# Attention and two expert layers in one kernel: four chunks ahead instead of two, and gathers in another order

## The chip, the cores and the metric

One core of a Trainium2 chip runs the whole kernel in one launch. The metric is the device time of one execution in microseconds (us), as the median of several. The engines are named as in the profile: PE is TensorE (matrix products; PEld is its loading of weights), DVE is VectorE, ACT is ScalarE, POOL is GpSimd, and SP is the engine whose queue issues the plain transfers.

## The reference

Three parts follow one another; each takes the result of the one ahead.

```python
# 1 sliding-window attention: 4 batches, 8 heads, 576 positions, head 64, window 64
scores = np.where(mask, scale * (q @ k.T), -1e9)     # mask: 0 <= i - j < 64
x = softmax(scores) @ v                              # -> x, 2304 tokens x 512
# 2 "moe": one dense layer
h = x @ w_in                                         # 512 -> 2048
x = (h - np.tanh(h)) @ w_out                         # 2048 -> 512
# 3 "moe2": eight experts, each token goes to one
logits = xn @ en.T / tau                             # normalised rows, 8 experts
e, gate = argmax(logits), softmax(logits)[argmax]
out = gate * (np.maximum(x @ w1[e], 0) @ w2[e])      # 512 -> 1024 -> 512
```

w_in and w_out come as 64-bit floating-point words, so a block of them takes twice the bytes and has to be decoded on the chip.

## The kernel before

Products are made of 32-bit numbers that are split into a high and a low part: one product of the reference becomes three on TensorE (`mm3`: high by high, high by low, low by high; lines 596 to 598). The splitting is work of its own: a copy to the high part (L222, on ScalarE or VectorE) and a subtraction for the low part (L572 for x, L393 and L862 for weights, L662 for the hidden layer).

The 2304 tokens lie in nine chunks of 256 (`CT`). Attention (`t_attn`) runs in units of half a chunk, n = 0 to 17; its result is x transposed. For the chunks in `direct` it goes straight into a buffer of pool "x" on the chip (two such buffers); for every other visit of a chunk it is spilled to `xTd` in DRAM (L552) and later loaded again (`t_xload`, L581) into one of four staging buffers "st", and split.

The dense layer has 16 blocks of 128 hidden units (`KF`). A *slot* is one chunk by one block: 12 products of 128x256 (`mm1`: x by w_in) and 6 of 128x512 (`mm2`: hidden layer by w_out). `t_moe1` takes two blocks, a *pair*, at once: `mm1`, then a chain of five ScalarE and five VectorE operations (VectorE's are L635, L644, L648, L652 and last the low part L662), then `mm2`. The weights of a block stay in one of 16 "w" slots until all chunks that use it have passed; loading and decoding a block (`t_decode`: loads L345 and L350, five VectorE operations L364, L367, L373, L378, L393 on each half) goes on during the first stage, and so does attention. Since the weights of the early stage are not there at once, the list `order` visits the first four chunks in pieces, (chunk, first block, last block), and puts away partial sums between: `t_sum` loads the sum so far (L687), adds (L694), and stores it (L699) to `part`. Chunks 4 to 8 then go through all 16 blocks. After its last block a chunk is routed (`t_route`, L700 to L844): it writes its rows to `x2d` and, for each token, its place in the list of its expert, `lst`.

The experts follow in an order that the chip works out. For each there is a first block of 256 tokens ("v" buffers) and an overflow block ("g" buffers): `t_list` loads the list of tokens (L1177 for the overflow part, L1179 for the first), `t_gather` gathers their rows on GpSimd (L908, two gathers of 128 rows a block), `t_xin` and `t_xin1` transpose them on TensorE (L931, L1030) and split them, `t_p1` and `t_ffn` do the products, `t_out` scatters (L1017). The overflow block stands in a branch on the token count. The counts are read into registers by eight `values_load` (L1280), one for each expert, on all engines.

No loop of the program sets the order: `Sched` takes all tasks with their engine, cost and due time (`prio`) and simulates them while the program is built; what its clock says is ready goes out, earliest due time first. It writes one list of instructions for each engine. Its costs for transfers (`SAME[DMA]`, `MOVED`) and the slot times `TC` and `TM` set what it believes, and so the order.

Of the kernel before, what the change touches and what calls it, by code (L numbers as in the profile page):

```python
# [40 lines left out]
class Sched:  # L41
# [3 lines left out]
    SAME = {PE: 0.0, ACT: 0.14, DVE: 0.13, POOL: 0.15, DMA: 0.91}  # L45
    OTHER, MOVED = 0.21, 0.91
# [51 lines left out]
    def run(self):  # L98
# [11 lines left out]
        while ready or ending:  # L110
            for i, (prio, n, alts, deps, bufs, allocs, lat, _) in enumerate(ready):
# [18 lines left out]
                if e == DMA:  # L130
                    issue = self.ISSUE_HALF if dur == HALF else self.ISSUE
                    self.free[e] = self.now + issue
                    end = self.moved = max(self.moved, self.now + issue + 0.65) + dur
# [28 lines left out]
def attn_moe_moe2(ctx, tc, q, k, v, w_in, w_out, emb, tau, w1, w2, out):  # L162

    nc = tc.nc
# [234 lines left out]

    def t_attn(n, pr, direct, spill):  # L400

# [136 lines left out]
        if direct:  # L538
            if p == 0:
                xT[c] = Buf("x")  # L540
# [17 lines left out]
    def t_split(x, part, src, key, d0, d1, pr, psum):  # L558
# [3 lines left out]
        def hi():  # L562
            return x.t[:, 0, d0:d1, :].rearrange("p a b -> p (a b)")

        def lo():
            return x.t[:, 1, d0:d1, :].rearrange("p a b -> p (a b)")
# [33 lines left out]
    def t_moe1(c, f, acc, first, last, pr):  # L600
# [4 lines left out]
        def mm1(i):  # L605
            w = wt[f + i]
            for d in range(KD):
# [3 lines left out]
                    hp.t[:, i * CT:(i + 1) * CT], w.t[:, s], w.t[:, s2], x.t[:, 0, d, :], x.t[:, 1, d, :],  # L611
# [612 lines left out]
    T0, TC, TM = 8, 4.5, 3.3  # L1224
# [6 lines left out]
    order = [(0, 0, 4), (1, 0, 4), (1, 4, 8), (0, 4, 8), (2, 0, 8), (3, 0, 8), (3, 8, 12), (2, 8, 12)]  # L1231
    order += [(2, 12, KF), (3, 12, KF), (0, 8, KF), (1, 8, KF)]
    order += [(c, 0, KF) for c in range(4, NC)]
    direct = (0, 1)
    AHEAD = 25
    start, due, load, held, s_ = {}, {}, [], [], 0
    for c, f0, f1 in order:
        load.append(c not in held and not (c in direct and f0 == 0))
        held = [x for x in held if x != c][-1:] + [c]
# [4 lines left out]
    t_weights(lambda f, o: due[f] - 6.0 + 3.0 * o)  # L1244
    for n in range(NC * NU):
        c = n // NU
        t_attn(
            n, min(TA * n, slot_t(start[c, 0]) - AHEAD + 5.0 * (n % NU)) if c else 1.0 * n, c in direct,
            any(l and x[0] == c for l, x in zip(load, order)),
        )  # L1250
    for (c, f0, f1), l in zip(order, load):
        if l:
            t_xload(c, slot_t(start[c, f0]) - 15.0)
# [5 lines left out]
        x2 = t_sum(c, acc, f0 > 0, f1 == KF, f1 - 5, end - 12.0 if c + 1 < NC else 0.0)  # L1259
# [12 lines left out]
    t_list(0, 1, fin - 50)  # L1272
    t_list(1, 0, fin - 49)
    t_counts(fin)
    blk_o = t_gather(lb[:, 0, 1], ("lb", 0, 1), "g", fin)
    blk_n = t_gather(lb[:, 1, 0], ("lb", 1, 0), "v", fin)
# [163 lines left out]
```

## Time and profile before

| | |
|---|---|
| median of 3 runs | 871.47 us (869.81 to 877.52) |
| the profiled execution | 870.94 us, its span 869.2 us |
| mean granted clock of TensorE | 0.97 of full speed |
| PE, PEld busy | 789.5 us (91%), 685.9 us (79%) |
| DVE, ACT busy | 592.5 us (68%), 502.3 us (58%) |
| POOL busy | 94.1 us (11%) |
| instructions | 15603 |
| moved | 107.2 MB, 123 GB/s |

An engine's busy time is the time in which the profiler saw at least one of its instructions at work. TensorE's products overlap, so the next one starts well ahead of the end that is shown. Where a row of the timeline has a bracket, the engine was idle for that long ahead of it, and the name behind the arrow is what ended the wait. In the view by stretches the columns are: the stretch, its length, busy time and number of instructions (x) of PE, PEld, DVE, ACT and POOL, the granted clock of TensorE as a share of full speed, the busy share of the DMA engines, and GB/s. About the first 330 us hold attention and the decoding of weights beside the dense layer, up to about 560 the dense layer is alone, and from then on the experts run.

### The profile page before, as it was taken

To read this page: it belongs to the slowest core of one execution; us is meant where nothing else is said; L and a number is where in the kernel's file an instruction comes from. 1 tells how busy PE (TensorE), PEld (TensorE's weight loads), DVE (VectorE), ACT (ScalarE), POOL (GpSimd) and SP (SyncE) were. 2 spreads that over 40 slices of the span, in tenths; PEclk is the share of its full clock that TensorE was granted. 3 is DMA by queue.
4 is the path that set the end of the run, shared out by engine and by line. 5 is a ranking of instruction groups with operands and counts; after the bars stand their busy time and mean duration, and the time that the engine had idled before them with its cause. 6 is when DMAs were issued, how large, how long until landed. Compare 5 with 4: busy or idle time off the path is not lost. (4 is left out here: it accounts for less than half of the span.)

```text
span 869.2 us, 15603 instructions
## 1 busy us (share of the span) xinstructions
PE 789.5 (91%) x5703; PEld 685.9 (79%) x5703; DVE 592.5 (68%) x1459; ACT 502.3 (58%) x1165; POOL 94.1 (11%) x116
## 2 busy tenths in 40 slices
PE   4687889999998999999999998895989999997995
PEld 3576678887987889899898987675879788886884
DVE  6998999999986796767667677951276377253721
ACT  6998798788955775656555556821244344242421
POOL 2000000000020110010101001022022123121210
PEclk9988899999999999999999999996999999998999
DMA  8964765447425310100100006615066266235411
GB/s 267 300 198 129 260 219 174 145 133 259 136 63 113 111 60 15 50 1 5 44 2 26 1 25 216 179 45 168 13 227 209 100 221 226 93 92 175 157 38 39
DMA packets 66284, 107.20 MB, mean 123 GB/s; under 512 B 8452, under 2 KB 44292, under 8 KB 66192
## 3 DMA queue, kind: packets, MB, share of 16 engines
q1 hardware_dynamic: 61296, 92.88, 33.1%
q0 software_dynamic: 4896, 13.13, 5.0%
q8 instruction: 53, 0.87, 0.5%
q14 instruction: 39, 0.32, 0.1%
HBM read 87.47 MB, written 19.56 MB: 123 GB/s over the span
## 5 line engine op out<-in xcount | busy, mean ns | idle before, releaser
L596 PE MATMUL h<-x,w 128*128 128x256 f32 x776 | 224.6, 289 | 10.0 <-DVE g L648 7.7
L598 PE MATMUL h<-x,w 128*128 128x256 f32 x776 | 221.4, 285 | 1.5 <-DVE w L393 1.5
L597 PE MATMUL h<-x,w 128*128 128x256 f32 x776 | 221.2, 285 | 1.2 <-DVE x L572 1.2
L596 PE MATMUL o<-w,gh 128*128 128x512 f32 x464 | 188.2, 406 | 11.2 <-ACT gh L658 10.2
L598 PE MATMUL o<-w,gh 128*128 128x512 f32 x464 | 184.5, 398 | 5.6 <-DVE gh L662 3.1
L597 PE MATMUL o<-w,gh 128*128 128x512 f32 x464 | 183.1, 395 | 0.0
L596 PEld LDWEIGHTS h<-x,w 128*128 128x128 f32 x776 | 149.9, 193 | 18.3 <-issue 9.8
L597 PEld LDWEIGHTS h<-x,w 128*128 128x128 f32 x776 | 150.0, 193 | 5.0 <-DVE x L572 1.4
L598 PEld LDWEIGHTS h<-x,w 128*128 128x128 f32 x776 | 150.0, 193 | 2.2 <-DVE w L393 2.1
L598 PEld LDWEIGHTS o<-w,gh 128*128 128x128 f32 x464 | 87.9, 189 | 33.5 <-DVE gh L662 7.6
L596 PEld LDWEIGHTS o<-w,gh 128*128 128x128 f32 x464 | 88.3, 190 | 29.5 <-ACT gh L658 11.2
L222 ACT CAST w<-st 128x512 fp32r<-128x512 f32 x140 | 83.0, 628 | 32.0 <-DMA st<-in_moe_w_dram 28.8
L597 PEld LDWEIGHTS o<-w,gh 128*128 128x128 f32 x464 | 88.4, 191 | 13.9
L862 DVE TENSOR_TENSOR w<-st,w 128x512 fp32r<-128x512 f32 x128 | 82.0, 686 | 6.0 <-ACT w L222 5.7
L658 ACT CAST gh<-g 128x512 fp32r<-128x512 f32 x72 | 44.3, 621 | 51.5 <-DVE g L652 46.6
L640 ACT ACTIVATE g<-h 128x512 f32<-128x512 f32 x72 | 43.1, 599 | 47.0 <-DVE g L644 42.0
L648 DVE TENSOR_TENSOR g<-h,g 128x512 f32<-128x512 f32 x72 | 49.6, 688 | 27.7 <-ACT g L640 26.9
L635 DVE SCALAR_TENSOR_TENSOR g<-g 128x512 f32<-128x512 f32 x72 | 49.9, 693 | 20.8 <-ACT g L627 20.4
L662 DVE TENSOR_TENSOR gh<-g,gh 128x512 fp32r<-128x512 f32 x72 | 49.3, 690 | 16.2 <-ACT gh L658 16.2
L644 DVE TENSOR_TENSOR g<-h,g 128x512 f32<-128x512 f32 x72 | 49.8, 691 | 9.9 <-ACT g L640 5.6
L482 ACT ACTIVATE pr<-pr,mx 128x128 f32<-128x128 f32 x144 | 56.2, 398 | 0.0
L652 DVE COPY_PREDICATED g<-big,g 128x512 f32<-128x512 uint16 x72 | 53.8, 748 | 1.0
(171 smaller groups left out, 1156.2 us busy)
## 6 DMA issues: line engine op xcount, KB each, us to landing
st<-in_moe_w_dram SPq DMA_DIRECT2D x64, 512.0 KB, 5.2
st<-in_moe_w_in_dram SPq DMA_DIRECT2D x16, 512.0 KB, 4.8
st<-in_moe_w_out_dram SPq DMA_DIRECT2D x16, 512.0 KB, 3.6
v<-in_v_dram SPq DMA_DIRECT2D x16, 512.0 KB, 5.1
k<-in_k_dram SPq DMA_DIRECT2D x16, 320.0 KB, 5.2
q<-in_q_dram SPq DMA_DIRECT2D x18, 256.0 KB, 4.0
xTd<-tmp SPq DMA_DIRECT2D x18, 256.0 KB, 4.2
st<-xTd SPq DMA_DIRECT2D x9, 512.0 KB, 4.4
```

The source lines that it names most:

```text
L222: return {ACT: (act, lambda: nc.scalar.copy(out=o(), in_=i())), DVE: (dve, lambda: nc.vector.tensor_copy(out=o(), in_=i()))}
L482: nc.scalar.activation(out=pr_.t[:, i, :], in_=pr_.t[:, i, :], func=AF.Exp, bias=st["m"][:, i:i + 1], scale=-1.0, accum_out=st["den"][:, i ...
L596: nc.tensor.matmul(out=ps, lhsT=ah, rhs=bh, start=start, stop=False)
L597: nc.tensor.matmul(out=ps, lhsT=ah, rhs=bl, start=False, stop=False)
L598: nc.tensor.matmul(out=ps, lhsT=al, rhs=bh, start=False, stop=stop)
L635: {DVE: (0.6, lambda: nc.vector.scalar_tensor_tensor(out=sq(), in0=sq(), scalar=SQ_B, in1=u(), op0=ALU.add, op1=ALU.mult))},
L644: {DVE: (0.6, lambda: nc.vector.tensor_tensor(out=sq(), in0=hp.t, in1=sq(), op=ALU.mult))},
L648: {DVE: (0.6, lambda: nc.vector.tensor_tensor(out=u(), in0=hp.t, in1=u(), op=ALU.subtract))},
L652: {DVE: (0.6, lambda: nc.vector.copy_predicated(out=sq(), mask=big.t.bitcast(DT.uint16), data=u()))},
L658: {ACT: (0.52, lambda: nc.scalar.copy(out=gh(), in_=sq()))}, reads=[(g, 1), (acc[0], "-"), (acc[1], "-")],
L662: {DVE: (0.6, lambda: nc.vector.tensor_tensor(out=gl(), in0=sq(), in1=gh().bitcast(F32), op=ALU.subtract))},
L862: return lambda: eng.tensor_tensor(out=w.t[:, b], in0=raw.t[:, a], in1=w.t[:, a].bitcast(F32), op=ALU.subtract)
```

## The change

Four chunks instead of two are worked on over the first four weight blocks with their x still on the chip. Chunks 0 and 1 have the two "x" buffers, chunks 2 and 3 take two of the 16 "w" slots for it, which `xv` views in the shape of x. After those four blocks the x of chunks 2 and 3 goes on to the second four, then 1 and 0; the third and fourth four blocks are visited in an order in which two chunks reload their x from `xTd` each time. The sums of the four chunks are put away more often: 12 stores and 12 loads of partial sums, where there were 8 of each. x is loaded nine times and spilled 18 times in both programs.

In the planner a transfer takes 1.2 times its duration and lands 1.5 after instead of 0.91; the slot times `TC` and `TM` are shorter, attention is due 10 ahead of its slot instead of 25, and x is loaded 12 ahead instead of 15. The gathers of expert 0 and 1 are asked for in another order: list and rows of expert 1's first block ("v") ahead of expert 0's overflow ("g"). One `values_load_multi_w_load_instructions` of all eight counts, planned as a task, stands where eight `values_load` followed the first part of the program.

```diff
-    SAME = {PE: 0.0, ACT: 0.14, DVE: 0.13, POOL: 0.15, DMA: 0.91}
-    OTHER, MOVED = 0.21, 0.91
+    SAME = {PE: 0.0, ACT: 0.14, DVE: 0.13, POOL: 0.15, DMA: 1.5}
+    OTHER, MOVED = 0.21, 1.5
...
-                    end = self.moved = max(self.moved, self.now + issue + 0.65) + dur
+                    end = self.moved = max(self.moved, self.now + issue + 0.65) + 1.2 * dur
...
+    def xv(x):
+        return x.t.rearrange("p (h k t) -> p h k t", h=2, k=KD) if x.pool == "w" else x.t
...
-                xT[c] = Buf("x")
+                xT[c] = Buf(direct)
...
-                    hp.t[:, i * CT:(i + 1) * CT], w.t[:, s], w.t[:, s2], x.t[:, 0, d, :], x.t[:, 1, d, :],
+                    hp.t[:, i * CT:(i + 1) * CT], w.t[:, s], w.t[:, s2], xv(x)[:, 0, d, :], xv(x)[:, 1, d, :],
...
-    T0, TC, TM = 8, 4.5, 3.3
+    T0, TC, TM = 8, 3.7, 2.9
...
-    order = [(0, 0, 4), (1, 0, 4), (1, 4, 8), (0, 4, 8), (2, 0, 8), (3, 0, 8), (3, 8, 12), (2, 8, 12)]
-    order += [(2, 12, KF), (3, 12, KF), (0, 8, KF), (1, 8, KF)]
-    order += [(c, 0, KF) for c in range(4, NC)]
-    direct = (0, 1)
-    AHEAD = 25
-    start, due, load, held, s_ = {}, {}, [], [], 0
-    for c, f0, f1 in order:
-        load.append(c not in held and not (c in direct and f0 == 0))
-        held = [x for x in held if x != c][-1:] + [c]
+    order = [(0, 0, 4, "x"), (1, 0, 4, "x"), (2, 0, 4, "w"), (3, 0, 4, "w"), (3, 4, 8, ""), (2, 4, 8, "")]
+    order += [(1, 4, 8, ""), (0, 4, 8, ""), (0, 8, 12, ""), (1, 8, 12, ""), (3, 8, 12, "load"), (2, 8, 12, "load")]
+    order += [(2, 12, KF, ""), (3, 12, KF, ""), (1, 12, KF, "load"), (0, 12, KF, "load")]
+    order += [(c, 0, KF, "load") for c in range(4, NC)]
+    AHEAD, LEAD, WLEAD = 10, 12.0, 6.0
+    start, due, s_ = {}, {}, 0
+    for c, f0, f1, how in order:
...
+        first = [x[3] for x in order if x[0] == c]
         t_attn(
             n, min(TA * n, slot_t(start[c, 0]) - AHEAD + 5.0 * (n % NU)) if c else 1.0 * n,
...
+            first[0] if first[0] != "load" else None, "load" in first,
         )
...
-            t_xload(c, slot_t(start[c, f0]) - 15.0)
+        if how == "load":
+            t_xload(c, slot_t(start[c, f0]) - LEAD)
...
-        x2 = t_sum(c, acc, f0 > 0, f1 == KF, f1 - 5, end - 12.0 if c + 1 < NC else 0.0)
+        x2 = t_sum(c, acc, f0 > 0, f1 == KF, f1 - 5 if f1 - 5 > f0 else f0, end - 12.0 if c + 1 < NC else 0.0)
...
-    t_list(0, 1, fin - 50)
-    t_list(1, 0, fin - 49)
+    t_list(1, 0, fin - 50)
+    t_list(0, 1, fin - 49)
     t_counts(fin)
-    blk_o = t_gather(lb[:, 0, 1], ("lb", 0, 1), "g", fin)
     blk_n = t_gather(lb[:, 1, 0], ("lb", 1, 0), "v", fin)
+    blk_o = t_gather(lb[:, 0, 1], ("lb", 0, 1), "g", fin + 2.0)
+    vals = []
+    SC.add(
+        {DVE: (0.3, lambda: vals.extend(
+            nc.values_load_multi_w_load_instructions(cnti[0:1, 0:E], min_val=0, max_val=NT)[1]))},
+        reads=[("cnt", 0), ("ids", blk_o[0][0])], prio=fin + 30.0,
+    )
...
-    vals = [nc.values_load(cnti[0:1, e:e + 1], min_val=0, max_val=NT) for e in range(E)]
```

In the changed program the lines of the kernel's body stand four to eight further down (L662 is L666, L699 is L703, L908 is L912).

GpSimd's list at the change from expert 0 to expert 1, before: `lst` is the lists' store, v the first block of expert 1, g the overflow of expert 0, `out_dram` the scatter of the result.

```order
L844 DMA lst<-pg,su 18432x2 x2
L908 DMA g_6863<-x2d,gi 128x512
L908 DMA g_6871<-x2d,gi 128x512
L908 DMA v_6877<-x2d,gi 128x512
L908 DMA v_6879<-x2d,gi 128x512
L1017 DMA out_dram<-pr_6873,ids 2304x512
L1017 DMA out_dram<-pr_6875,ids 2304x512
L1280 TENSOR_LOAD cnti x8
```

The same place after the change:

```order
L848 DMA lst<-pg,su 18432x2 x2
L912 DMA v_6875<-x2d,gi 128x512
L1283 TENSOR_LOAD cnti
L912 DMA v_6965<-x2d,gi 128x512
L912 DMA g_6967<-x2d,gi 128x512
L912 DMA g_6973<-x2d,gi 128x512
L1021 DMA out_dram<-pr_6969,ids 2304x512
L1021 DMA out_dram<-pr_6971,ids 2304x512
```

The v gathers have moved ahead of the g gathers, and one register load, between the two v gathers, has taken the place of eight behind the scatters.

TensorE's list at the same place, before: the last transposes of v, the eight register loads, the branch on the count, and the transposes of g inside it.

```order
L931 MATMUL a_6890<-ident,v_6877 128x128
L931 MATMUL a_6890<-ident,v_6879 128x128
L931 MATMUL a_6890<-ident,v_6877 128x128
L931 MATMUL a_6890<-ident,v_6879 128x128
L1280 TENSOR_LOAD cnti x8
L1299 COMPARE_AND_BRANCH
L1030 MATMUL a_7017<-ident,g_6863 128x128 x4
```

After the change, the register load stands here (o is the last sum of expert 0, gh its hidden layer):

```order
L600 MATMUL o_6669<-w_6425,gh_6845 128x512
L601 MATMUL o_6669<-w_6425,gh_6845 128x512
L602 MATMUL o_6669<-w_6425,gh_6845 128x512
L1283 TENSOR_LOAD cnti
L600 MATMUL o_6668<-w_6425,gh_6869 128x512
L601 MATMUL o_6668<-w_6425,gh_6869 128x512
L602 MATMUL o_6668<-w_6425,gh_6869 128x512
L600 MATMUL o_6669<-w_6425,gh_6869 128x512
L601 MATMUL o_6669<-w_6425,gh_6869 128x512
L602 MATMUL o_6669<-w_6425,gh_6869 128x512
L935 MATMUL a_6978<-ident,v_6875 128x128
L935 MATMUL a_6978<-ident,v_6965 128x128
```

The register load has moved ahead of the last six products of expert 0, and the transposes of v follow these.

VectorE's list up to the low part of the 26th pair (gh), before: routing of a chunk (L797 to L839) among the pair's own operations.

```order
L806 TENSOR_SCALAR se<-se 128x2
L807 RECIPROCAL pg<-se 128x2
L808 COPY pg<-tok 128x2
L648 TENSOR_TENSOR g_3254<-h_3188,g_3254 128x512
L829 TENSOR_TENSOR sl<-a_3313,oh 128x16
L832 TENSOR_REDUCE sf<-sl 128x2
L833 CAST su<-sf 128x2
L839 TENSOR_TENSOR cum<-cum,oh 128x8 x2
L652 COPY_PREDICATED g_3254<-big_3255,g_3254 128x512
L222 COPY pT_3342<-a_3341 128x512
L222 COPY pT_3351<-a_3350 128x512
L662 TENSOR_TENSOR gh_3357<-g_3254,gh_3357 128x512
```

The same place after the change, up to the 26th low part:

```order
L373 SCALAR_TENSOR_TENSOR tmp_2992<-st_2939,tmp_2992 128x512
L393 TENSOR_TENSOR w_2555<-st_2675,w_2555 128x512
L378 SCALAR_TENSOR_TENSOR st_2939<-st_2939,tmp_2992 128x512
L648 TENSOR_TENSOR g_3022<-h_2890,g_3022 128x512
L652 TENSOR_TENSOR g_3022<-h_2890,g_3022 128x512
L393 TENSOR_TENSOR w_2790<-st_2939,w_2790 128x512
L656 COPY_PREDICATED g_3022<-big_3023,g_3022 128x512
L576 TENSOR_TENSOR x_3026<-st_3025,x_3026 128x512 x2
L639 SCALAR_TENSOR_TENSOR g_3088<-g_3088 128x512
L666 TENSOR_TENSOR gh_3110<-g_3022,gh_3110 128x512
```

Where routing stood there are now the last decoding operations of the weights (L373, L378, L393) and a low part of a reloaded x (L576); the routing comes later.

SP's list where the sums of the dense layer are put away, before: `part` is the partial sum of a chunk, st a staging buffer, q and k the inputs of attention, and the in_moe rows are weights.

```order
L421 DMA v_2187<-in_v_dram 128x4x256
L552 DMA xTd<-tmp_2220 128x2x256
L699 DMA part_76<-st_2237 128x1024
L411 DMA q_2298<-in_q_dram 128x2x256
L415 DMA k_2301<-in_k_dram 128x2x320
L687 DMA st_2305<-part_76 128x1024
L350 DMA st_2376<-in_moe_w_out_dram 128x1024
L345 DMA st_2417<-in_moe_w_in_dram 128x4x256
```

After the change, in the stretch in which the first four chunks are put away:

```order
L556 DMA xTd<-tmp_2230 128x2x256
L691 DMA st_2251<-part_74 128x1024
L585 DMA st_2327<-xTd 128x4x256
L703 DMA part_74<-st_2251 128x1024
L691 DMA st_2394<-part_74 128x1024
L350 DMA st_2405<-in_moe_w_out_dram 128x1024
L345 DMA st_2416<-in_moe_w_in_dram 128x4x256
L703 DMA part_74<-st_2394 128x1024
```

A load of x and a second put-away have come in between, and a store of `part_74` stands directly ahead of a load of the same sum.

## Rows read from the trace of the kernel before

**Rows 1.** Busy time of each engine by stretch (columns as explained above)
```profile
0.00:130.00 130.00, 96.70 (x1067) 80.18 (x1068) 112.71 (x378) 109.36 (x341) 7.87 (x35) 0.92 0.72 230
130.00:260.00 130.00, 127.13 (x1000) 112.04 (x1000) 122.82 (x294) 102.47 (x241) 5.54 (x5) 1.00 0.48 152
260.00:330.00 70.00, 67.29 (x615) 58.04 (x616) 52.79 (x157) 45.59 (x118) 7.39 (x7) 1.00 0.34 93
330.00:520.00 190.00, 189.67 (x1238) 169.89 (x1237) 130.13 (x249) 111.46 (x194) 12.35 (x12) 1.00 0.06 18
580.00:605.00 25.00, 15.20 (x71) 12.96 (x71) 5.35 (x12) 3.22 (x6) 5.88 (x6) 0.73 0.46 148
605.00:870.00 265.00, 240.68 (x1393) 208.17 (x1391) 120.41 (x263) 92.53 (x196) 48.61 (x46) 0.97 0.40 130
```

**Rows 2.** Timeline of DVE: low parts of the 6th, 26th and 34th pair
```profile
120.88 1.29 DVE L662 TENSOR_TENSOR gh<-g,gh 128x512 fp32r<-128x512 f32 x2
...
259.43 0.68 DVE L662 TENSOR_TENSOR gh<-g,gh 128x512 fp32r<-128x512 f32 x1
...
323.68 0.69 DVE L662 TENSOR_TENSOR gh<-g,gh 128x512 fp32r<-128x512 f32 x1
```

**Rows 3.** Timeline of DVE in an expert: four 512-wide operations in a row
```profile
662.43 2.49 DVE L862 TENSOR_TENSOR w<-st,w 128x512 fp32r<-128x512 f32 x4
```

**Rows 4.** Waits of DVE from 260 to 330: total, times, longest
```profile
DVE g L635 <- ACT g L627: 4.0, 4, 1.9
DVE x L222 <- DMA st<-xTd: 3.7, 1, 3.7
```

**Rows 5.** Timeline of PE: score products, then spacing of the other products
```profile
306.67 1.10 PE L457 MATMUL a<-k,q 64*64 64x128 f32 x32
...
505.71 0.39 PE L598 MATMUL o<-w,gh 128*128 128x512 f32 x1
505.93 0.28 PE L596 MATMUL h<-x,w 128*128 128x256 f32 x1
506.05 0.28 PE L597 MATMUL h<-x,w 128*128 128x256 f32 x1
```

**Rows 6.** View of one line: L699 (stores of partial sums), then L581
```profile
DMA to landing us min/median/max: 2.6/3.3/5.9
...
DMA to landing us min/median/max: 3.7/4.4/8.8
```

**Rows 7.** Timeline of PE at the change from expert 0 to 1
```profile
591.42 0.45 PE L931 MATMUL a<-ident,v 128*128 128x128 f32 x1 [5.75 <-DMA v<-x2d,gi]
593.86 1.75 PE L931 MATMUL a<-ident,v 128*128 128x128 f32 x7 [1.99 <-DMA v<-x2d,gi]
597.66 1.09 PE L1030 MATMUL a<-ident,g 128*128 128x128 f32 x4 [2.05 <-issue]
598.40 0.56 PE L596 MATMUL a<-x,w 128*128 128x256 f32 x1
```

**Rows 8.** Timeline of POOL at the same place
```profile
584.95 0.98 POOL L908 DMA_INDIRECT g<-x2d,gi  x1 [6.01 <-DVE ids L902]
...
587.51 0.95 POOL L908 DMA_INDIRECT v<-x2d,gi  x1 [0.30 <-issue]
```

**Rows 9.** View of one line: L1280, on TensorE's queue
```profile
L1280 PEldq TENSOR_LOAD <-cnti x8: 300/307/493, 593.9 to 597.0; - x8
```

**Rows 10.** Timeline of DVE at the same place: the split of x
```profile
596.25 1.28 DVE L572 TENSOR_TENSOR x<-a,x 128x512 fp32r<-128x512 f32 x2
```

**Rows 11.** Expert 1 to 2: timeline of POOL, then of PE
```profile
633.71 0.98 POOL L908 DMA_INDIRECT v<-x2d,gi  x1 [0.30 <-DVE w L222]
...
641.17 0.30 PE L931 MATMUL a<-ident,v 128*128 128x128 f32 x1 [1.71 <-DMA v<-x2d,gi]
642.26 0.98 PE L931 MATMUL a<-ident,v 128*128 128x128 f32 x7 [0.78 <-DMA v<-x2d,gi]
```

**Rows 12.** Waits of PE from 605 on: total, times, longest
```profile
PE o L598 <- DVE gh L978: 2.4, 6, 0.5
```

More of the change, by code (lines that the diff above doesn't have):

```diff
@@ L562, in hi @@
         def hi():
-            return x.t[:, 0, d0:d1, :].rearrange("p a b -> p (a b)")
+            return xv(x)[:, 0, d0:d1, :].rearrange("p a b -> p (a b)")
         def lo():
-            return x.t[:, 1, d0:d1, :].rearrange("p a b -> p (a b)")
+            return xv(x)[:, 1, d0:d1, :].rearrange("p a b -> p (a b)")
         act = 0.48 if psum else 0.52
@@ L1243, in attn_moe_moe2 @@
         s_ += f1 - f0
-    t_weights(lambda f, o: due[f] - 6.0 + 3.0 * o)
+    t_weights(lambda f, o: due[f] - WLEAD + 3.0 * o)
     for n in range(NC * NU):
         c = n // NU
+        first = [x[3] for x in order if x[0] == c]
         t_attn(
-            n, min(TA * n, slot_t(start[c, 0]) - AHEAD + 5.0 * (n % NU)) if c else 1.0 * n, c in direct,
-            any(l and x[0] == c for l, x in zip(load, order)),
-        )
-    for (c, f0, f1), l in zip(order, load):
-        if l:
-            t_xload(c, slot_t(start[c, f0]) - 15.0)
+            n, min(TA * n, slot_t(start[c, 0]) - AHEAD + 5.0 * (n % NU)) if c else 1.0 * n,
+            first[0] if first[0] != "load" else None, "load" in first,
+        )
+    for c, f0, f1, how in order:
+        if how == "load":
+            t_xload(c, slot_t(start[c, f0]) - LEAD)
         acc = [Buf("o") for _ in range(2)]
```

## The prediction

> **What bounds the kernel now.** I read the stretches first [rows 1]. By the table above TensorE is busy 789 of 869 us, yet that says little, because a product shown as 0.28 us gives way to the next after 0.12 [rows 5]. What a change can win is idle or stretched time, so I looked at where that lies. From 330 to 520 TensorE is busy 189.67 of 190 us: nothing is to be had there. From 0 to 130 it is busy 96.7 us, from 580 to 605 only 15.2 of 25, and from 605 on it lacks 24 of 265.
>
> Then I read VectorE beside it. From 130 to 260 VectorE is busy 122.8 of 130 us, and there the low part (L662), its last step for a block pair, is what TensorE's second products need. The 6th low part ends at 122.2, the 26th begins at 259.43, the 34th at 323.68 [rows 2]. Twenty pairs in 137 us, 6.9 us a pair, while TensorE needs for a pair 24 products of 128x256 at 0.12 and 12 of 128x512 at 0.22 [rows 5], 5.5 us, plus attention. So VectorE sets the pace up to about 260, and from 260 to 330 it is busy only 52.8 of 70 [rows 1]: there it waits for ScalarE and once, 3.7 us, for a load of x from DRAM [rows 4].
>
> The second place is the change from expert 0 to expert 1. TensorE stands 5.75 us and then 1.99 for gathered rows, and 2.05 for nothing that the profile names [rows 7].
>
> **The change part by part.** *First stage.* From the two orders I counted what stands on VectorE ahead of the 34th low part. A 512-wide operation follows the one ahead by 0.60 us (four in 2.49, the last of them 0.69) [rows 3]. Added: 8 additions of partial sums (16 become 24), +4.8; 4 low parts of x, +2.4; 3 plain copies of partial sums, +1.8. Gone from ahead of it: 7 copies of attention outputs, 4.3; some attention 1.6 and routing 1.5; other kinds add 0.9. Net +2.5 us. The decoding of weights is 160 operations in both; of it less lies ahead of the 6th pair (65 instead of 88), which is given back by the 26th.
>
> Now the idle time. Between the 26th and the 34th low part, 64.3 us, VectorE's own work fills 51.5 on this count, so it is idle 12.8 us there. In the new order VectorE has about 60.7 us of work between the 26th and the 34th low part (236.3 to 297.0 in the running sum), while TensorE has 54.9. So VectorE should be the late engine to the end of this stretch and have no reason to idle; it keeps only the 17 us that it idles before the 26th pair (260.1 less a running sum of 243.0). I take the 34th low part at 324.4 + 2.5 - 12.8 = 314.1.
>
> TensorE, however, has then done less: 12 products of 128x256 (1.4 us) and 32 score products, 16 transposes and 32 value products stand behind that point instead of ahead. By [rows 5] 32 score products take 1.10, as many value products about the same, and 16 transposes at the 0.12 of a product 1.9; together with the first 1.4 that is 5.5 us that must follow. From there TensorE was full [rows 1], so the stage gains 324.4 - 314.1 - 5.5 = **-4.8**. Bounds: with 5 us less idle than now in the early part, -9.8; with all of the 12.8 still there, +8.0.
>
> The x of chunks 2 and 3 stays in weight slots, but these two are loaded later again, as are 1 and 0: nine loads and 18 spills in both programs, so this removes no traffic; it removes a wait at the first visit. The longer transfer times in the planner only move issues. New are four stores and four loads of partial sums, 512 KB each; a store lands after 3.3 us [rows 6]. They stand on SP's queue, and at one place a store is directly followed by the load of the same sum, so that SP waits there for the landing, and the weight loads and the attention inputs queued behind it wait too. I cost this at nothing, since DMA engines are less than half busy from 130 on [rows 1] and the weight blocks are loaded ahead; without that cover it is one landing each.
>
> *Expert 0 to 1.* GpSimd issues g, g, v, v, the first at 584.95, the third at 587.51 [rows 8]; TensorE waits for v. With v first, and one load of the counts between, the second v is issued 2.5 - 0.3 = 2.2 us earlier, and so the eight transposes end that much earlier. Behind them TensorE ran eight register loads at about 0.3 [rows 9], which is the 2.05 us; one load is left and stands ahead of the last six products of expert 0. That does not give the whole 2.05: the next products of 128x256 (598.40) need x, whose split on VectorE ends at 597.53, 1.9 us after the last transpose (595.61) [rows 7, 10]. So 2.8 us between the transposes and those products become 1.9. Together 2.2 + 0.9 = **-3.1**. Bounds: -2.0 if the g rows, now last, hold the branch, and -5.0 if the idle time goes whole and some of the slow products with it: the granted clock is 0.73 in this stretch [rows 1], so shorter gaps may also give faster products.
>
> The trace shows a load of one register at 0.3 us [rows 9]. The Trainium skill, page DMA: Bandwidth & Descriptors, section "Latency and other measured facts", gives about 600 ns as its floor; by that the seven loads removed would be 4.2 us and the sum 2 us lower; the trace says half of it.
>
> *Expert 1 to 2.* The order was g, v, v, g: a g stands ahead of the first v (633.71), and a gather holds GpSimd some 1.3 us (two from 584.95 to 587.51) [rows 8, 11]. TensorE waits 1.71 and 0.78 for v. With v, v first I take **-1.5** (0 if the list is what is late, -2.5 for both waits). The later experts keep g, v, v, g.
>
> *Inside the experts.* In the new order up to nine weight operations stand in a row on VectorE ahead of one low part of the hidden layer (L978), five before; elsewhere fewer. The six waits of this kind are 2.4 us in all [rows 12]. I take **-0.4**, between -2.4 and +3.
>
> The sum: -4.8 - 3.1 - 1.5 - 0.4 = -9.8 against 870.94, the profiled execution, of which 869.2 is the span: **861.1**. The median of the runs is 871.47, half a microsecond above, which changes nothing here.
>
> **The rivals.** *A, the first stage gains more.* If the early part, with 23 decoding operations fewer ahead of the 6th pair, also saves 5 us of VectorE's idle time, the stage gives -9.8 and the time is about 856; for it speaks that TensorE lacks 33 us of the first 130 [rows 1], against it that attention and transfers (0.72 busy) set much of that. *B, the first stage gives nothing.* VectorE has more work in the whole stage, 12 us on my count, and was already the late engine; if 5 us of idle time come back in the stretch from 260 to 330, only the experts' -5.0 is left: 866. The waits for ScalarE there [rows 4] speak for it. The Trainium skill, page Perfetto Trace Analysis, section "Identifying the Most-Contended Engine", says to work on the engine of highest occupancy first; by that nothing would come of adding to VectorE to relieve no TensorE work, which the trace supports between 130 and 260. *C, slower.* All 12.8 us of idle time stay, since SP's round trips for partial sums (3.3 a store) push the loads of x, which already took up to 8.8 to land [rows 6], and VectorE waits for x as it did once [rows 4]. The stage is then +8.0, and with the experts' -5.0 the time is 874; from two more such waits of 3.7 on the path it is 881. It decides where a reloaded x lands later than its pair is due. *D, the change does not do what it says:* the gathers wait for the lists and not for each other, so that the order of v and g is worth nothing, and the stage comes out as forecast: 870.9 - 4.8 - 0.4 = 866.
>
> **How the numbers follow.** The forecast 0.5, A 0.2, B 0.15, C 0.1, D 0.05. About 1%, 8.7 us, is what a measurement of this kernel can tell from no change, so faster means below 862.8. Of the forecast's own spread (856 to 867) six in ten lie there, and all of A: 0.3 + 0.2, with a little of B: 0.53. C gives 0.05 to slower and 0.05 to within 1%; same is 0.42. The range goes from 850, where all the lower bounds together end (870.9 - 9.8 - 5.0 - 2.5 - 2.4 = 851), to 873, short of C.
>
> **What the profile of the changed kernel would show.** The 34th low part near 314 instead of 324, and VectorE idle under 8 us from 260 to 314; TensorE full until 510 and finishing the first stage about 5 us earlier; at the change to expert 1, v issued ahead of g, gaps of TensorE of some 6.5 us in all instead of 9.8 and none named "issue"; less than 1 us before the transposes of expert 2. I would be wrong if VectorE waits for x or for partial sums from DRAM between 260 and 330, if SP stands at stores of partial sums while weights are late, or if the longest gap at expert 1 stays near 5.8.

## The result and the profile after

The changed kernel takes 861.24 us (median of 4 runs, 857.9 to 861.96) against 870.64 in the same comparison; the ratio is 0.9891, 95% interval 0.9851 to 0.993. It is faster by about 9 us. Timed again later (e16), it came to 856.76 us and a ratio of 0.9828 (0.9787 to 0.9869). The ratios leave out single runs that lie over 1.5% above the fastest of their kernel, the medians do not. The profiled execution took 861.28 us, its span 859.5.

The stretches of the changed kernel, with the columns of [rows 1]:

```profile
0.00:130.00 130.00, 103.19 (x1094) 87.44 (x1095) 118.91 (x366) 103.00 (x304) 7.14 (x35) 0.95 0.69 215
130.00:260.00 130.00, 123.67 (x949) 109.27 (x948) 125.42 (x287) 102.18 (x235) 0.71 (x1) 0.99 0.58 188
260.00:330.00 70.00, 67.50 (x594) 57.86 (x593) 53.11 (x180) 43.77 (x121) 11.33 (x11) 0.98 0.40 97
330.00:520.00 190.00, 185.73 (x1287) 165.90 (x1286) 128.67 (x267) 110.65 (x207) 11.24 (x11) 1.00 0.07 23
580.00:605.00 25.00, 17.82 (x89) 14.95 (x88) 5.34 (x13) 4.57 (x9) 5.87 (x6) 0.80 0.45 147
605.00:860.00 255.00, 235.43 (x1366) 204.46 (x1364) 123.79 (x275) 84.15 (x179) 47.30 (x46) 0.97 0.42 135
```

TensorE is busy 6.5 us more in the first 130 us and 4 us less between 330 and 520, where it had been full. The low parts of the 6th, 26th and 34th pair on VectorE's timeline (L666 is L662 of before), to be held against [rows 2]:

```profile
101.76 1.25 DVE L666 TENSOR_TENSOR gh<-g,gh 128x512 fp32r<-128x512 f32 x2
...
243.78 0.68 DVE L666 TENSOR_TENSOR gh<-g,gh 128x512 fp32r<-128x512 f32 x1
...
310.51 0.69 DVE L666 TENSOR_TENSOR gh<-g,gh 128x512 fp32r<-128x512 f32 x1
```

They end at 103.0, 244.5 and 311.2 instead of 122.2, 260.1 and 324.4. Up to here the first stage is 13 us ahead. The 66th low part ends at 515.8 instead of 516.4, and the last product of expert 0 at 584.8 instead of 585.7: nearly all of the lead is gone by then. Some 4 us of it went to waits, the rest to work of TensorE that stands behind the 34th pair. What TensorE waits for between 312 and 520 (in total, times, longest; before the whole list was one wait of 0.3 us):

```profile
PE h L600 <- DVE g L652: 3.2, 2, 1.6
PE a L751 <- ACT st L222: 0.9, 1, 0.9
```

The change to expert 1 on TensorE's timeline, beside [rows 7]:

```profile
587.67 0.45 PE L935 MATMUL a<-ident,v 128*128 128x128 f32 x1 [2.91 <-DMA v<-x2d,gi]
589.53 1.76 PE L935 MATMUL a<-ident,v 128*128 128x128 f32 x7 [1.41 <-DMA v<-x2d,gi]
593.29 1.08 PE L1034 MATMUL a<-ident,g 128*128 128x128 f32 x4 [2.00 <-DMA g<-x2d,gi]
```

and what GpSimd issues there (v is the first block of expert 1, g the overflow of expert 0), beside [rows 8]:

```profile
583.89 0.98 POOL L912 DMA_INDIRECT v<-x2d,gi  x1 [7.93 <-DVE gi L905]
585.32 0.96 POOL L912 DMA_INDIRECT v<-x2d,gi  x1 [0.45 <-issue]
586.59 0.95 POOL L912 DMA_INDIRECT g<-x2d,gi  x1 [0.30 <-issue]
```

The gaps are 2.91, 1.41 and 2.00 instead of 5.75, 1.99 and 2.05; the third is now a wait for the g rows. Behind expert 1, the waits of TensorE from 605 on, of which [rows 12] has the one that mattered:

```profile
PE a L600 <- issue: 5.1, 1, 5.1
PE a L935 <- DMA v<-x2d,gi: 2.2, 2, 1.7
...
PE o L600 <- ACT gh L978: 0.3, 1, 0.3
```

The six waits for VectorE's low part of the hidden layer (2.4 us) are gone, and the waits for gathered rows are 2.2 us instead of 4.1. At the change to expert 2 there is none. From the first product inside the branch of expert 0 (598.40 in [rows 7], 594.0 now) to the end it took 270.8 us before and 265.5 now, for the same products.

### The profile page after: what moved, and what is told of

Its sections match the earlier page's. It is cut to its first block, busy times and chain, and to the rows that moved or that the text cites. A ratio compares the mean times of both kernels' runs of the same rounds, so it can differ in the third digit from the quotient of the medians.

```text
span 859.5 us, 15577 instructions
## 1 busy us (share of the span) xinstructions
PE 788.2 (92%) x5703; PEld 687.3 (80%) x5703; DVE 604.9 (70%) x1498; ACT 483.3 (56%) x1121; POOL 89.8 (10%) x116
## 5 line engine op out<-in xcount | busy, mean ns | idle before, releaser
L600 PE MATMUL h<-x,w 128*128 128x256 f32 x712 | 206.6, 290 | 10.0 <-DVE g L652 9.4
L601 PE MATMUL h<-x,w 128*128 128x256 f32 x712 | 203.5, 286 | 2.0 <-DVE x L576 1.9
L602 PE MATMUL h<-x,w 128*128 128x256 f32 x712 | 203.0, 285 | 0.3 <-DVE w L393 0.2
L600 PEld LDWEIGHTS h<-x,w 128*128 128x128 f32 x712 | 137.8, 194 | 17.6 <-issue 9.7
L601 PEld LDWEIGHTS h<-x,w 128*128 128x128 f32 x712 | 138.0, 194 | 6.1 <-DVE x L576 2.7
L602 PEld LDWEIGHTS h<-x,w 128*128 128x128 f32 x712 | 137.8, 194 | 0.8 <-DVE w L393 0.8
L222 ACT CAST w<-st 128x512 fp32r<-128x512 f32 x116 | 70.2, 629 | 33.1 <-DMA st<-in_moe_w_dram 21.4
L644 ACT ACTIVATE g<-h 128x512 f32<-128x512 f32 x72 | 42.9, 596 | 38.2 <-DVE g L648 31.6
L627 ACT ACTIVATE g<-h 128x512 f32<-128x512 f32 x72 | 42.6, 594 | 36.9 <-PE h L602 31.6
L662 ACT CAST gh<-g 128x512 fp32r<-128x512 f32 x72 | 44.1, 616 | 33.6 <-DVE g L656 29.4
L978 ACT ACTIVATE gh<-h 128x256 fp32r<-128x256 f32 x50 | 19.1, 383 | 73.3 <-PE h L602 54.8
```

Source lines behind the costliest of these rows:

```text
L222: return {ACT: (act, lambda: nc.scalar.copy(out=o(), in_=i())), DVE: (dve, lambda: nc.vector.tensor_copy(out=o(), in_=i()))}
L600: nc.tensor.matmul(out=ps, lhsT=ah, rhs=bh, start=start, stop=False)
L601: nc.tensor.matmul(out=ps, lhsT=ah, rhs=bl, start=False, stop=False)
L602: nc.tensor.matmul(out=ps, lhsT=al, rhs=bh, start=False, stop=stop)
L627: {ACT: (0.48, lambda: nc.scalar.activation(out=u(), in_=hp.t, func=AF.Square))},
L644: {ACT: (0.48, lambda: nc.scalar.activation(out=u(), in_=hp.t, func=AF.Tanh))},
```

## The experiments

Each kernel is compared with the kernel before on the same chip, as a ratio with its 95% interval. Where the profiles are compared, I use three points of TensorE's timeline that every kernel has: the end of expert 0's last product, the first product of 128x256 in its branch (*P*), and the end of the span. In the diffs `...` stands for lines left out.

**e1_boundary: only the lists, gathers and count load.** The order on each engine ahead of the change to expert 1 and behind it is that of before.

```diff
-    t_list(0, 1, fin - 50)
-    t_list(1, 0, fin - 49)
+    t_list(1, 0, fin - 50)
+    t_list(0, 1, fin - 49)
     t_counts(fin)
-    blk_o = t_gather(lb[:, 0, 1], ("lb", 0, 1), "g", fin)
     blk_n = t_gather(lb[:, 1, 0], ("lb", 1, 0), "v", fin)
+    blk_o = t_gather(lb[:, 0, 1], ("lb", 0, 1), "g", fin + 2.0)
+    vals = []
+    SC.add(
+        {DVE: (0.3, lambda: vals.extend(
+            nc.values_load_multi_w_load_instructions(cnti[0:1, 0:E], min_val=0, max_val=NT)[1]))},
...
-    vals = [nc.values_load(cnti[0:1, e:e + 1], min_val=0, max_val=NT) for e in range(E)]
```

> The kernel before with only the new lists, gathers and the one count load; its first stage keeps the order of before, instruction by instruction. The profile after shows TensorE losing 3.4 us less from the end of expert 0 to the first product of the branch, and 2.6 us less at the change to expert 2. Theory: both belong to this edit, so the time is about 6 us below before, near 865, and the wait for gathered rows at expert 1 falls from 5.75 to about 3 us, the one at expert 2 from 1.71 to nothing. Rival: the gain at expert 2 comes from something else in the changed program (the other order of weight copies); then about 867.

Measured: 1.0013 (0.9994 to 1.0032), no gain; both expectations fell. Its TensorE timeline at the change to expert 1:

```profile
588.07 0.45 PE L931 MATMUL a<-ident,v 128*128 128x128 f32 x1 [4.17 <-DMA v<-x2d,gi]
592.12 1.75 PE L931 MATMUL a<-ident,v 128*128 128x128 f32 x7 [3.61 <-DMA v<-x2d,gi]
594.95 1.09 PE L1030 MATMUL a<-ident,g 128*128 128x128 f32 x4 [1.07 <-DMA g<-x2d,gi]
```

The first gap is shorter, the second longer (3.61 instead of 1.99): the rows of the first v gather now come early, those of the second not. It is issued at 585.75 instead of 588.77, but TensorE uses its rows 6.4 us later, where before it took 5.1 and in the changed kernel 4.2; why, I did not find. P comes at 595.9, 2.5 us earlier than before. That is not the edit's doing, though: the 72nd and last low part of the dense layer ends at 558.2 in this profile and at 560.0, 559.3 and 561.5 in before, e11 and e14, with the same lists up to there, so some 2 us of the 2.5 are spread between executions. From the end of expert 0 to P it takes 12.05 us instead of 12.2 to 12.7 in those three. The rest takes 275.4 us instead of 270.8; 2.9 us of this are longer waits for gathered rows (7.0 against 4.1 in all), and at the change to expert 2 the wait of 1.77 us is still there.

**e2_stage: the changed kernel with the old lists, gathers and eight count loads.**

```diff
-    t_list(1, 0, fin - 50)
-    t_list(0, 1, fin - 49)
+    t_list(0, 1, fin - 50)
+    t_list(1, 0, fin - 49)
...
+    blk_o = t_gather(lb[:, 0, 1], ("lb", 0, 1), "g", fin)
...
+    vals = [nc.values_load(cnti[0:1, e:e + 1], min_val=0, max_val=NT) for e in range(E)]
```

> The changed kernel with the lists, gathers and eight count loads of before; the first stage is that of the changed kernel. Theory: the first stage was worth only 1 to 2 us by its end, so 868 to 870, with the 34th low part at 311 and a lead of about 6 us there that is gone by the 66th pair. Rival, the prediction's own: the stage is worth 4.8 us, so about 866.

Measured: 0.9852 (0.9807 to 0.9896), the whole gain, more than either expected. Its expert 0 ends at 585.7, as before, and P comes at 596.3, 2.1 us earlier; the greater part of the gain lies behind P, 260.5 us to the end. Its lists there differ from those of before, although nothing of the experts' code is changed: the planner's transfer times hold for them too.

**e8_oldplan, e10_steady, e4_olddma: four chunks, but with planning numbers of before.** e4 takes back the transfer times (the edit shown), e10 these and TM (3.3), e8 also TC (4.5) and the due times (25 and 15).

```diff
-    SAME = {PE: 0.0, ACT: 0.14, DVE: 0.13, POOL: 0.15, DMA: 1.5}
-    OTHER, MOVED = 0.21, 1.5
+    SAME = {PE: 0.0, ACT: 0.14, DVE: 0.13, POOL: 0.15, DMA: 0.91}
+    OTHER, MOVED = 0.21, 0.91
...
-                    end = self.moved = max(self.moved, self.now + issue + 0.65) + 1.2 * dur
+                    end = self.moved = max(self.moved, self.now + issue + 0.65) + dur
```

> The changed kernel with all planning numbers of before (transfer times, TC, TM, due times of attention and of loads of x); four chunks, two of them in weight slots, and the new boundary stay. TensorE's list goes back to a steady two first products, one second product per block from the 36th pair on, where the changed kernel has groups of five first products in a row. Theory: the lead at the 34th pair comes from the order of segments and the loss after it from the groups of five, so the stage keeps about 5 us: near 857. Rival A: the lead at the 34th pair comes from the new planning numbers, and without them it is gone: 864 or more. Rival B: the loss between the 34th and the 66th pair is VectorE's added work and stays: about 861.

> The changed kernel with only the transfer times of before and TM 3.3; TC 3.7 and the new due times of attention and x stay. The list on TensorE is steady from the 40th pair on. Theory (groups of five first products make TensorE wait for the two buffers of the hidden layer): about 4 us of loss between the 34th and the 66th pair go away, near 857. Rival: the order is not what costs, 861, with as much loss between the 34th and the 66th pair (8 us) as in the changed kernel.

> The changed kernel with the transfer times of before; TC, TM and due times stay as changed. Experts as before, and a first stage planned with short transfers. The two other four-chunk stages planned so ended 7 to 9 us later than that of the changed kernel. Theory: the longer transfer times are what makes the four-chunk order no slower, so 872 to 880. Rival: TC and TM did that, and the stage stays as in the changed kernel: about 869.

Measured: 1.0019 (0.9995 to 1.0043), 1.0084 (1.0052 to 1.0116) and 1.0118 (1.0078 to 1.0159). The first two do have no wait of TensorE at all between 333 and 527, and their lists there have no groups of first products for five blocks in a row; the changed kernel, e4 and e9 have such groups and wait 3.2 to 6.3 us there for the hidden layer's buffers. But that is worth less than what the old numbers lose ahead of it: expert 0 ends at 592.6, 594.3 and 599.6. Rival A of e8 holds: the 34th low part comes at 329.2, and the lead is gone. Both expectations of e10 fell (879.44 us). Of e4 the theory holds, that the longer transfer times are what makes the four-chunk order no slower; at 884.06 us it lost even more than the 872 to 880 expected.

**e9_plan_only: the kernel before with all new planning numbers.** The same numbers as above, put into the kernel before.

> The kernel before with all planning numbers of the changed one; segments of two chunks, gathers and count loads stay. Its experts have the lists of the changed kernel, its first stage is planned anew. Theory: gain of the experts, and a first stage like the one of before: 862 to 865. Rival: the new numbers only suit the four-chunk order, and with two chunks the stage is 5 us or more longer: 868 or more.

Measured: 0.9918 (0.9888 to 0.9948), 866.43 us. Expert 0 ends at 592.4, some 7 us later than before, so the rival is right for the first stage; behind P it takes only 260.4 us, so the theory is right for the experts.

**e11_exp_new: longer transfer times for experts 1 to 7 only**, in the kernel before, and **e12_exp_old**, the reverse in the changed kernel (there 0.91, 0.91 and 1.0). `XDUR` is the factor on a transfer's duration.

```diff
+    XDUR = 1.0
...
-                    end = self.moved = max(self.moved, self.now + issue + 0.65) + dur
+                    end = self.moved = max(self.moved, self.now + issue + 0.65) + self.XDUR * dur
...
+    SC.SAME, SC.MOVED, SC.XDUR = {**SC.SAME, DMA: 1.5}, 1.5, 1.2
     for e in range(E):
         t0 = SC.now
```

> The kernel before; only from expert 1 on the planner uses the longer transfer times. First stage and the change to expert 1 stay instruction by instruction as before, and the lists of experts 1 to 7 become those of the changed kernel (VectorE's low parts ahead of weight work, v, v, g, g at expert 2). Theory after the first four runs: the whole gain lies in this, since TensorE lost 34 to 40 us behind the change to expert 1 with the old lists and 25 to 30 with the new ones: about 8 us, near 864. Rival: only the 2.6 us at expert 2 belong to it and the rest differs from run to run: about 870.

> The changed kernel; only from expert 1 on the planner uses the transfer times of before, so the first stage is that of the changed kernel and the lists of experts 1 to 7 are those of before. Theory: the gain goes, about 869 to 871. Rival (the first stage carries the gain, as forecast): about 864.

Measured: e11 0.9885 (0.9847 to 0.9923), 862.52 us: the first theory held, and this one edit gives as much as the whole change in its first comparison. e12 0.9924 (0.9896 to 0.9953), 865.39 us: 6.6 us of the gain stay, nearer to the rival: more than half of the gain of the first comparison, less than half of that of the second. The waits of TensorE in e11 from 605 on, the whole list:

```profile
PE a L932 <- DMA v<-x2d,gi: 3.6, 4, 1.6
PE a L597 <- issue: 3.2, 1, 3.2
PE a L597 <- DVE x L1041: 1.0, 1, 1.0
PE a L1077 <- ACT tmp L1066: 0.8, 3, 0.3
PE h L597 <- PEq L1311: 0.5, 1, 0.5
```

No wait for the hidden layer is left. One place in expert 1 shows how. Before, on ScalarE, VectorE and TensorE (L974 is the high part of the hidden layer, L978 the low part, L862 and the copies L222 are weights):

```profile
671.45 2.29 ACT L222 CAST w<-st 128x512 fp32r<-128x512 f32 x4
673.65 0.38 ACT L974 ACTIVATE gh<-h 128x256 fp32r<-128x256 f32 x1
...
674.44 0.39 ACT L974 ACTIVATE gh<-h 128x256 fp32r<-128x256 f32 x1
...
674.92 1.89 DVE L862 TENSOR_TENSOR w<-st,w 128x512 fp32r<-128x512 f32 x3
676.73 0.42 DVE L978 SCALAR_TENSOR_TENSOR gh<-h,gh 128x256 fp32r<-128x256 f32 x1
...
677.21 0.50 PE L598 MATMUL o<-w,gh 128*128 128x512 f32 x1 [0.48 <-DVE gh L978]
```

The same two parts in e11 (its lines stand one further down):

```profile
670.92 0.38 ACT L975 ACTIVATE gh<-h 128x256 fp32r<-128x256 f32 x1 [2.68 <-PE h L599]
...
673.74 0.38 ACT L975 ACTIVATE gh<-h 128x256 fp32r<-128x256 f32 x1 [0.89 <-PE h L599]
...
671.33 0.42 DVE L979 SCALAR_TENSOR_TENSOR gh<-h,gh 128x256 fp32r<-128x256 f32 x1 [2.10 <-ACT gh L975]
671.84 1.90 DVE L863 TENSOR_TENSOR w<-st,w 128x512 fp32r<-128x512 f32 x3
674.15 0.43 DVE L979 SCALAR_TENSOR_TENSOR gh<-h,gh 128x256 fp32r<-128x256 f32 x1 [0.42 <-ACT gh L975]
```

Before, four copies of weights stand ahead of a high part on ScalarE, and three weight operations ahead of the low part at 676.73 on VectorE, whose high part was ready at 674.83; TensorE waits 0.48 us for it. In e11 both engines are idle ahead of these parts, and the weight work runs around them. The 2.49 us of weight operations in [rows 3] cost TensorE nothing: it does not wait for the low part behind them.

**e14_gather2: only the gathers at expert 2**, v, v, g, g instead of g, v, v, g, in the kernel before; no other engine's order changes.

```diff
-            blk_o = t_gather(lb[:, e, 1], ("lb", e, 1), "g", t0 + 3.0)
+            blk_o = t_gather(lb[:, e, 1], ("lb", e, 1), "g", t0 + 3.0, after=[(blk_n[0][1], 0)] if e == 1 else [])
```

> The kernel before with one pair of gathers moved: at the change to expert 2 both v ahead of the first g; all other lists stay as before. Theory: TensorE's two waits there (2.5 us) go and nothing else, so 868 to 869, and the other 6 us of the run with the experts planned anew come from the order of VectorE and ScalarE. Rival: gather order is the whole gain, about 863.

Measured: 0.9971 (0.994 to 1.0002), about 2.5 us, not quite clear of nothing. The rival is out; the theory is not shown. The wait at expert 2 is gone from the profile, but the time from P to the end is not shorter (270.6 us against 270.8): the waits for the hidden layer (the second and third row) have grown from 3.4 to 5.5 us:

```profile
PE a L596 <- issue: 5.2, 1, 5.2
PE o L596 <- ACT gh L974: 3.0, 5, 1.0
PE o L598 <- DVE gh L978: 2.5, 7, 0.5
PE a L931 <- DMA v<-x2d,gi: 1.4, 1, 1.4
```

**e7_double_add: VectorE's load in the first stage.** Each of the 24 additions of partial sums is followed by a maximum of the sum with itself; the result is the same.

```diff
-                alts = {DVE: (0.6, lambda i=i, h=h: nc.vector.tensor_tensor(
-                    out=x2.t[:, h], in0=acc[i].t, in1=x2.t[:, h], op=ALU.add))}
+                def add2(i=i, h=h):
+                    nc.vector.tensor_tensor(out=x2.t[:, h], in0=acc[i].t, in1=x2.t[:, h], op=ALU.add)
+                    nc.vector.tensor_tensor(out=x2.t[:, h], in0=x2.t[:, h], in1=x2.t[:, h], op=ALU.max)
+
+                alts = {DVE: (0.6, add2)}
```

> The changed kernel with a second 512-wide VectorE operation (a maximum of the sum with itself, which changes nothing) behind each of the 24 additions of partial sums; every other instruction keeps its place. It adds 24 times 0.60, 14.4 us, to VectorE up to the 34th pair. Theory of the prediction (VectorE sets the pace up to there and TensorE has no slack behind): the 34th low part moves from 311 to about 325 and the time to 873 to 876. Rival (VectorE idles enough beside TensorE, ScalarE and transfers to take it in): at most 5 us, 866 or less.

Measured: 873.57 us, 1.001 (0.998 to 1.0039), against 856.76 for the changed kernel on the same chip (**e16_changed_again**, no edit).

> The changed kernel once more, on the same chip as the last three, for comparison with them: 861, give or take 2.

It is 16.8 us slower, more than the 14.4 us expected, but just what was added: the 24 maxima take 0.69 us each in the trace, 16.6 us, and all stand ahead of the 34th low part. The 34th low part, in e7 and then in e16:

```profile
323.52 0.68 DVE L666 TENSOR_TENSOR gh<-g,gh 128x512 fp32r<-128x512 f32 x1
```

```profile
306.88 0.69 DVE L666 TENSOR_TENSOR gh<-g,gh 128x512 fp32r<-128x512 f32 x1
```

It moved by 16.6 us, and the end of expert 0 by 15.6 (597.3 against 581.7). VectorE is not busy throughout (from the 6th low part to the 34th it idles 12.4 us in e16 and 12.5 in e7), but none of that time took in the added work: it does set the pace.

**e13_steady_late: a steady rhythm from chunk 4 on**, by a rule that a pair's first products wait, in the plan, for the second products of the pair two back.

```diff
+        past.append(("mm2", c, f + 1))
+        back = past[-1 - 2:-2] if c >= 4 else []
...
-                {PE: (1.44, lambda i=i: mm1(i))}, reads=[(wt[f + i], 0), (wt[f + i], 2), *xkeys(c)], writes=[(hp, i)],
+                {PE: (1.44, lambda i=i: mm1(i))}, reads=[(wt[f + i], 0), (wt[f + i], 2), *xkeys(c), *back], writes=[(hp, i)],
```

> The changed kernel, with one more rule for the planner: from chunk 4 on the first products of a pair wait in the plan for the second products of the pair two back. TensorE's list is that of the changed kernel up to the 31st pair and steady from then on; experts unchanged. Theory (groups of five first products wait for the two buffers of the hidden layer): of the 8.3 us that TensorE loses between the 34th and the 66th pair some 5 go away, so 856 to 857, faster than both kernels. Rival: the loss there is VectorE's added work or the reloading of x, and stays: 861.

Measured: 867.74 us, 0.9915 (0.9883 to 0.9947), slower than the changed kernel; both expectations fell. TensorE's waits from 316 to 520:

```profile
PE o L602 <- DVE gh L670: 2.1, 3, 0.8
PE o L600 <- ACT gh L666: 1.9, 9, 0.4
```

The waits for the two buffers are gone and others have come, for the hidden layer's high and low part. Before, one and a half pairs of further first products stand between the first and the second products of a pair; my rule left one, and the chain of ScalarE and VectorE then ends just after TensorE gets there. So this run tells nothing of a steady list with the old distance. These waits are not all that it lost, either: expert 0 ends at 595.3, and ahead of that TensorE waits 4.25 us for gathered rows at 546, which I did not look into.

## Why the forecast came out right

The total was right, 861.1 forecast and 861.24 measured, and so was the sign; the make-up of the sum was not. That the total came so near is luck: the first stage gave less than forecast, the experts much more, and the second comparison of the same kernel lies 4 us lower. From the profiles (end of expert 0, and P):

| kernels | first stage | boundary | end of expert 0 | P | P to the end |
|---|---|---|---|---|---|
| before, e11, e14 | old | old | 585.7, 585.0, 587.2 | 598.4, 597.5, 599.4 | 270.8, 263.5, 270.6 |
| e1 | old | new | 583.9 | 595.9 | 275.4 |
| e2 | new | old | 585.7 | 596.3 | 260.5 |
| changed, e16, e12 | new | new | 584.8, 581.7, 583.4 | 594.0, 591.4, 592.8 | 265.5, 260.8, 271.7 |

*First stage, -4.8.* VectorE sets the pace up to the 34th pair, which e7 shows, and that pair came at 311.2 where 314.1 was forecast. But the idle time was not won where the prediction had it. The stretches up to the 26th low part and from there to the 34th, before and then after:

```profile
0.00:260.11 260.11, 223.94 (x2068) 192.33 (x2070) 235.64 (x672) 211.95 (x581) 13.41 (x40) 0.96 0.60 191
260.11:324.37 64.26, 61.55 (x579) 52.79 (x576) 49.62 (x151) 42.44 (x113) 5.58 (x6) 1.00 0.34 92
```

```profile
0.00:244.46 244.46, 211.31 (x1937) 182.99 (x1938) 229.51 (x605) 190.74 (x498) 7.14 (x35) 0.97 0.64 203
244.46:311.20 66.74, 64.25 (x537) 54.83 (x537) 56.14 (x188) 48.90 (x135) 10.05 (x10) 0.97 0.52 131
```

VectorE's work is the same in sum (285.3 and 285.6 us), its idle time is 13.5 us less. 9.5 us of that lie ahead of the 26th pair, where the prediction kept all of an idle time that it put at 17 us (it was 24.5); only 4.0 lie behind it, where the prediction took away all of 12.8 (it was 14.6, and 10.6 are left). So the time of the 34th pair is right by luck, too. One of the prediction's signs of being wrong did show: at 289 VectorE waits 2.5 us for the high part of a reloaded x, and ScalarE ahead of it 3.4 for its load from DRAM:

```profile
288.69 0.62 ACT L222 CAST x<-st 128x512 fp32r<-128x512 f32 x1 [3.44 <-DMA st<-xTd]
...
289.34 0.69 DVE L576 TENSOR_TENSOR x<-st,x 128x512 fp32r<-128x512 f32 x1 [2.49 <-ACT x L222]
```

The sentence that failed is "From there TensorE was full". From the 34th to the 66th low part it took 204.6 us instead of 192.0. 3.9 us of that are waits: the new list has groups of first products for five blocks after chunk changes, and TensorE waits 3.2 us there for the buffers of the hidden layer, and 0.9 for ScalarE. The other 8.7 are work, where 5.5 was counted: 64 score products, 16 transposes and 64 value products stand behind the 34th pair, not 32, 16 and 32. By P the stage is worth 2.1 us (598.4, the mean of three, less 596.3) to 3.2 (595.9 less 592.7, the mean of three). These are rough, as the same lists end expert 0 at 585.0 to 587.2 in one row of the table and at 581.7 to 584.8 in another. And the stage is worth anything only as a whole: four chunks with old numbers (e8) and two chunks with new numbers (e9) both end expert 0 some 7 us later than before.

*Stores and loads of partial sums, nothing.* SP does wait for them, in total, times and longest from 130 to 330:

```profile
SPq L703 <- DMA st<-part: 13.4, 3, 5.0
SPq L691 <- DMA part<-st: 9.2, 4, 3.8
```

No engine waits for a partial sum in that trace, so the cover held; the one late x was no more than before ([rows 4] has 3.7 us), and rival C did not come.

*Boundary, -3.1.* From the end of expert 0 to P it takes 9.3 us instead of 12.7 in the first profile, 3.4 less, near the forecast, but not by its terms. The transposes of v end 6.5 us behind expert 0 instead of 9.9, which is 3.4 where 2.2 was forecast. The 0.9 for the count loads did not come: P follows the last transpose of v by 2.7 us instead of 2.8, since TensorE now waits 2.00 us for the g rows, whose transposes stand ahead of P. The prediction had this case (the g rows hold the branch) only as a bound. And the worth of the boundary hangs on the stage ahead of it: with the old stage (e1) it is some 0.4 us, with the new one about 1.2 (10.6 us from the end of expert 0 to P in e2; 9.3, 9.7 and 9.4 in the changed kernel, e16 and e12). Alone (e1) it gave no time that could be measured. Of the one count load, I took the seven loads removed at 0.3 us each; the one that is left takes longer than any of them:

```profile
L1283 PEldq TENSOR_LOAD <-cnti x1: 778/778/778, 579.3 to 579.3; - x1
```

The Trainium skill, page DMA: Bandwidth & Descriptors, section "Latency and other measured facts", has about 600 ns as a floor; the trace has 0.31 for the middle one of eight loads in a row on this queue [rows 9] and 0.78 for the one that fetches all eight counts. The page and the trace differ, and the trace decides: a load in such a row takes half of that floor.

*Expert 1 to 2, -1.5, and inside the experts, -0.4.* Here the size was off by far: from P to the end seven kernels with the old lists take 269.3 to 275.5 us and seven with the new ones 258.5 to 265.5, about 10 us apart. The step that failed is "The longer transfer times in the planner only move issues". They also put the high and low parts of the hidden layer ahead of weight work where TensorE is waiting for them, 13 operations from ScalarE on VectorE (1472 instead of 1459 there), and v ahead of g at expert 2. e11 has all this alone and gains 10 us; e14 has the gathers alone, and its 2.5 are not clear of nothing. Whether the order of the parts or the 13 moved operations do the rest is not separated. Where the 10 us lie, the means of the seven profiles with the old lists and of the seven with the new ones show, from P to the end: TensorE's waits for the hidden layer are 4.1 us and 0.4, those for gathered rows 4.3 and 2.2, the unnamed wait near 790 is 4.8 and 3.5, all waits together 15.6 and 8.5; the other 3 us are shorter busy time of TensorE (247.5 and 244.4). I had counted the longest row of weight operations ahead of a low part, nine, and taken it for a cost. It is there, ahead of the third low part of an expert, which in e11 starts 2.4 us behind its high part (666.12); but TensorE does not wait for that one, and three of the other five low parts have one weight operation fewer ahead of them. The unnamed wait is 4.5 to 5.2 us in all seven profiles with the old lists, and 1.9 to 4.3 in six of the seven with the new ones (5.1 in the changed kernel); what ends it stays open.

*Rivals.* What the stage did lies between the forecast and B (nothing from it), but B's 866 was not reached because of the experts. That the order of v and g is worth nothing, as D had it, is what e1 measured for the boundary alone. The Trainium skill, page Perfetto Trace Analysis, section "Identifying the Most-Contended Engine", would start with TensorE, whose weight loading is busy 79% of the span before and VectorE 68%; e7 shows VectorE to be the one that binds up to the 34th pair, where 16.6 us more on VectorE are 16.8 us more in time.

The parts don't add up neatly. The timed ratios give the experts 10 us in one setting (e11) and 3 to 8 in the other (e12's ratio against the two of the changed kernel), the stage with the boundary 6 to 7 us (e12), and the two comparisons of the changed kernel themselves lie 5 us apart. By the profiles the experts' lists carry the larger part, 10 us against the 5.7 by which P comes earlier (598.4 to 592.7). The timed intervals are too wide to rank them: 6.7 to 13.3 us for the lists alone (e11), 4.1 to 9.1 for stage and boundary (e12). The boundary alone carries none that can be measured; the exact shares stay open.

## What to carry to other kernels

A planner's cost numbers are not local: one that is changed for one stage reorders every stage planned with it, so compare the lists of all stages, and above all of those that the change does not mention. When a change of several parts comes out as forecast, run the parts alone before believing the sum: here the larger part of the gain, by the profiles, came from the part that was forecast at 1.9 us. And where one engine is the late one, read off what it gives back downstream: a lead in the middle of the program is worth only what the lists behind it keep.

## Not expected

In a list of steady rhythm TensorE waits for next to nothing (0.3 us from 316 to 520) when one and a half further pairs stand between a pair's first and second products, and waits in every chunk when one pair does (e13, 4.0 us in all), although the engines' operations are the same. And one instruction that loads eight counts took 0.55 to 0.85 us on each engine, where eight loads of one took 0.27 to 0.32 each in the middle [rows 9 for TensorE], so that the saving on TensorE's queue was about 1.7 us (8 times 0.307 less 0.778) and not seven eighths of 2.5. P gained nothing from it in the changed kernel, since the g rows came no earlier.
